# Hedgehog attention and a ReGLU FFN on one Trainium2 core: gates between load bursts and crossbar turns, w_phi loaded by SyncE, and matmuls on zeros early on

## The chip, the cores and the metric

One NeuronCore of a Trainium2 chip runs the whole kernel. The metric is device time in microseconds (us) of one execution. The engines are TensorE (PE; PEld are its weight loads), VectorE (DVE), ScalarE (ACT), GpSimd (POOL) and SyncE (SP, which here only issues DMAs). Each engine works through its own list of instructions in order.

## What is computed

Attention with a learned feature map, over 8 batches of 8 heads, 576 positions and head dimension 64, and then a gated feed-forward net over all 4608 tokens:

```python
def phi(x):                                   # w_phi: 64 x 128
    proj = einsum('bhsd,df->bhsf', x, w_phi)
    proj = proj - max(abs(proj), axis=-1, keepdims=True)
    return concatenate([exp(proj), exp(-proj)], axis=-1)
q_p, k_p = phi(q), phi(k)
kv  = einsum('bhsf,bhsd->bhfd', k_p, v);  z = sum(k_p, axis=2)
num = einsum('bhsf,bhfd->bhsd', q_p, kv)
den = einsum('bhsf,bhf->bhs', q_p, z)[..., None] + 1e-06
x = (num / den)                               # to 4608 x 512
out = (maximum(x @ w_gate, 0) * (x @ w_val)) @ w_out     # 512 -> 1536 -> 512
```

Inputs and output are fp32; the kernel multiplies in bf16.

## The kernel before

**Stages.** For each batch the kernel loads k, q and v. The first 512 positions of a head are the "main" part (tiles kn, qn, vn), the last 64 are the "rest" (km, qm, vm). k and q must be turned (transposed) so that the head dimension lies on partitions. Batches 0 and 1 are turned on TensorE (`turn_pe`, L439, copied out of PSUM at L446), the others by DMA transposes through the crossbar, issued by SyncE (`turn_dma`, L454). TensorE projects the turned k with w_phi (L493 for pairs of heads, L539 for the rest). VectorE takes the largest magnitude of each row (L503), ScalarE the two exponentials (`exps`, L467). Since exp(proj - m) is exp(proj) times exp(-m), the k maxima are put on v instead: GpSimd scales v by them (`vs`, L518; rest `vsm`, L559, which for batch 0 can also go to VectorE). TensorE forms kv (`k_kv`, L586), with a column of scales beside v so that z comes with it. q is projected (L610), its maxima are found (L619; for batch 0 by a second projection with positions on partitions, L679, and a reduction L686), and q times kv is formed in `q_num` (L717). VectorE adds the two halves (L725, L732), takes the reciprocal (L742), GpSimd or VectorE divides (`xu`, L745), and xu is turned to xT (batch 0 on TensorE, L758 and L765, the others by SyncE).

**FFN.** There are nine groups: one for the main part of each batch, and a last one for all rests (`xT_mix`). Each group has 12 slices of the hidden dimension. For each, TensorE makes val (L787 with wv_sb) and gate (L787 with wg_sb), ScalarE copies val out of PSUM (L793), VectorE makes relu(gate) * val (L796). Then 4 x 12 products with wo_sb (L818) make four output tiles, copied at L828 and stored by SyncE at L833 (L837 for the rests). PSUM has 8 banks, handed out in a ring named `ps`.

**Order of the work.** Nothing runs in the order of the code. Every step is an `Op` with an engine or a choice of engines, an assumed duration, dependencies, buffers, and a key by which it ranks. `Plan.run` (L91) is a list scheduler that runs on the host when the program is built: it steps through assumed time, gives each free engine the ready step with the smallest key, and the order that comes out is the order in which each engine's instructions are written. Its assumptions decide only this order; on the chip semaphores decide when an instruction starts. Assumed durations, the added delays `LAT` and the factor of 1.8 on TensorE before `COLD` (L61, L173) are such assumptions.

**Loads and gates.** Loads of batch 0's k and v are issued by SyncE (L372, L386), the other loads mostly by GpSimd, which can convert fp32 to bf16 on the way. Batch 0's k arrives as fp32 in the space of wo_sb and is cast at L871: heads 0-1, 2-3, 4-7 and then the rest. w_phi is loaded twice by GpSimd (L335) into the two diagonal blocks of `w2`, whose other blocks VectorE clears (L341). Loads of batches 2 to 7 and all crossbar turns are marked `alone`: the planner starts a load only when it believes that SyncE's transfers have ended, and a turn only when it believes that GpSimd's have. A turn has besides a real wait (`gate`, set at L180, written at L1102) on the last GpSimd load planned before it. GpSimd's loads have no such wait on the turns. Loads of batch 0's q and of the first third of the FFN weights wait for k heads 4-7 (L895 to L902).

Of the kernel before, what the change touches and what calls it, by code (L numbers as in the profile page):

```python
# [18 lines left out]
class Buf:  # L19


    __slots__ = ("ring", "slot", "users", "free_at", "lock", "place")

    def __init__(self, ring):
        self.ring, self.slot, self.users, self.free_at, self.lock = ring, None, 0, 0.0, 0.0
        self.place = ring.made
        ring.made += 1
# [13 lines left out]
class Op:  # L41
    __slots__ = ("eng", "dur", "fn", "deps", "bufs", "banks", "key", "kind", "start", "end",
                 "land", "succ", "left", "ready", "bytes", "pad", "n", "inst", "alone", "gate", "tail", "bias")

    def __init__(self, eng, dur, fn, deps, bufs, banks, key, kind, nbytes, pad):
# [6 lines left out]
        self.succ, self.left, self.ready = [], 0, 0.0  # L52


class Plan:
# [3 lines left out]
    LAT = {PE: 0.26, ACT: 0.16, DVE: 0.2, POOL: 0.15, SP: 0.1}  # L59
    MARGIN = 0.2  # L60
    COLD = 14.0  # L61
# [29 lines left out]
    def run(self, quota):  # L91
        wait = {e: [] for e in (PE, ACT, DVE, SP, POOL)}
# [4 lines left out]
        last_load = None  # L97
# [9 lines left out]
        events = [0.0, 0.25, 0.75]  # L107
        order = []
        while left:
# [7 lines left out]
            while progress:  # L117
                progress = False
                for e in wait:
# [3 lines left out]
                    for o in wait[e]:  # L123
                        if o.start is not None or (best and o.key >= best.key):
                            continue
                        r = o.ready
# [5 lines left out]
                        if any(b.lock > now + 1e-9 for b in o.banks):  # L132
                            continue
# [20 lines left out]
                        if ok:  # L154
                            best = o
                    if best is None:
                        continue
# [15 lines left out]
                    if e == PE and now < self.COLD:  # L173
                        d *= 1.8
# [4 lines left out]
                    if o.alone and e == SP:  # L179
                        o.gate = last_load  # L180
# [11 lines left out]
                    for b in o.banks:  # L192
                        b.lock = o.land
# [10 lines left out]
                    for s in o.succ:  # L204
                        s.ready = max(s.ready, o.land)
                        s.left -= 1
                        if not s.left:
                            release(s)
                            heapq.heappush(events, max(s.ready, now))
# [12 lines left out]
def kernel(  # L222
# [16 lines left out]
    P = 128  # L239
# [68 lines left out]
    w2 = single("w2", [P, 2, F])  # L308

# [8 lines left out]
    op = plan.op  # L318

# [13 lines left out]
    def load_w():  # L333
        for hh in range(2):
            nc.gpsimd.dma_start(out=w2[D * hh : D * (hh + 1), hh, :], in_=w_phi)  # L335

    o_w = op(POOL, 1.3, load_w, key=(0, 0), pad=2.2)

    def clear_w():
        for hh in range(2):  # L340
# [40 lines left out]
    def load_rest_by_head(b, src, engname, key, tile_buf, deps=(), pad=0.0, dst=None):  # L381
        def go():
            v_ = src[b, :, SF:S, :].rearrange("(j x) p d -> x p j d", x=2)
            t = tile_buf.t if dst is None else dst
            for x in range(2):
                i = engines[engname].dma_start(out=t[SM * x : SM * (x + 1)], in_=v_[x])  # L386
            return i
# [5 lines left out]
    def load_rest_q(i, key, tile_buf, deps=(), pad=2.0):  # L393
        def go():
            for x in range(2):
                ins_ = nc.gpsimd.dma_start(
# [3 lines left out]
            return ins_  # L400
# [8 lines left out]
    SWITCH = 0.12  # L409
# [74 lines left out]
    def k_item(b, u, kT, turned, vn, o_v, key, dve_scale=False):  # L484
# [4 lines left out]
        def rows():  # L489
            for i in range(4):  # L490
# [7 lines left out]
        a = op(PE, 0.224 + SWITCH, rows, [*turned(2 * u), *turned(2 * u + 1), o_w],  # L498
               [kT, kp, m, e, vs], pair,
               key, "a")  # L500
        for x, ps in enumerate(pair):
# [31 lines left out]
    def k_rest(b, kmT, turned, vm, o_v, key, dve_scale=False):  # L533
# [22 lines left out]
        for x in range(2):  # L556
# [11 lines left out]
            sc.append(op(engs, {POOL: 1.12, DVE: 0.8}, scale, [o_e, o_v, o_clear], [vm, e, vs],  # L568
# [31 lines left out]
    def q_cols(hq, qT, turned, cols, dsts, mx, mdst, key):  # L600
# [6 lines left out]
        def go_cols():  # L607
            for x in range(2):
# [3 lines left out]
        a = op(PE, 0.222 + SWITCH, go_cols, [*turned, o_w],  # L612
               [qT, *{id(d[0]): d[0] for d in dsts}.values(), *([mx] if mx else [])], pair, key, "a")
        reds, exd = [], []
# [14 lines left out]
    def q_scale(mq, xq, zq, cq, n, deps, key):  # L629
# [34 lines left out]
        a = op(PE, 0.25, away, [*deps, o_consts], [mq, xq, zq, cq], [ps], key, "a")  # L664
        r = op(DVE, 0.2, amax, [a], [mq, xq], [ps], key, "a")
        z = op(DVE, 0.2, spread, [r, o_consts], [xq, zq], key=key, kind="a")
        b_ = op(PE, 0.2, back, [z], [zq], [ps], key, "a")
# [192 lines left out]
    W = C * D  # L860

# [16 lines left out]
    k_heads = ((0, 2), (2, 4), (4, 8))  # L878
    for i, (lo, hi) in enumerate(k_heads):
        o = load_main(0, "kn", k, SP, slice(lo, hi), (0, i), None, (), 0.0, kn32)  # L880
        last_k = o
        for u in range(lo // 2, hi // 2):
            c_ = cast(
                kn32[:, 2 * u : 2 * u + 2], lambda u=u: ins[0]["kn"].t[:, 2 * u : 2 * u + 2], 2 * W,
                [o], (2, 0, 0, u), ins[0]["kn"], (DVE, ACT),
            )
            got["kn", 0, 2 * u] = got["kn", 0, 2 * u + 1] = c_
    o = load_rest_by_head(0, k, SP, (0, 3), None, (), 0.0, km32)
    got["km", 0] = cast(km32, lambda: ins[0]["km"].t, NU * D, [o], (2, 0, 0, 5), ins[0]["km"],
# [247 lines left out]
```

## Time and profile before

| | |
|---|---|
| median of 4 runs | 405.69 us (405.07, 415.23, 404.29, 406.31) |
| the profiled execution | 405.07 us, of which its span is 403.3 us |
| TensorE clock granted over the span | 0.995 |
| busy: PE, DVE, ACT, POOL | 372.7, 262.0, 241.9, 165.3 us |
| FFN products L787 (wv, wg) and L818 | 95.6, 96.7 and 100.5 us |
| HBM read, written | 37.81 MB, 9.44 MB |

Times in the profile are counted from the span's start. "Busy" counts time in which at least one instruction of that engine was under way; matmuls overlap, so a group's busy time is less than its count times its mean. "Chain" is the chain of work that ended last, followed back from the end. A wait names the instruction that waited, what released it, and the total, the number of times and the longest, in us. In the timeline a row is a start, a length, an engine, a line and an operation with its count. A DMA's time to landing runs from its issue to its completion.

### The profile page before, as it was taken

How to read it: one execution, taken by the hardware profiler on the slowest of the kernel's cores; microseconds unless marked ns; L12 is line 12 of the kernel's file. 1: busy time of each engine (PE TensorE's matmuls, PEld its weight loads, DVE VectorE, ACT ScalarE, POOL GpSimd, SP SyncE). 2: the span in 40 equal slices, each digit the busy share in tenths (PEclk: the TensorE clock that was granted, in tenths of full speed). 3: DMA queues.
4: the chain of work that ended last, by engine and by line, in shares of the span. 5: the costliest groups of instructions: out<-in, count | busy, mean ns of one | idle time of the engine just before them, and what ended most of it. 6: DMA issues, size and time to landing. Idle time of an engine off the chain costs nothing.

```text
span 403.3 us, 8431 instructions
## 1 busy us (share of the span) xinstructions
PE 372.7 (92%) x3149; PEld 199.8 (50%) x3149; DVE 262.0 (65%) x648; ACT 241.9 (60%) x522; POOL 165.3 (41%) x196
## 2 busy tenths in 40 slices
PE   3687899989999999999899899989999999999995
PEld 2365588543643545364365436533654444444442
DVE  5879888298677789978975997378775311321420
ACT  5969985179639849878662795279713323323321
POOL 4864953149539625954963197345031000000000
PEclk9999899999999999999999999999999999999999
DMA  8999199490959964798696809581042001002004
GB/s 229 164 226 209 34 161 225 103 181 2 222 112 165 154 166 88 131 125 190 106 161 179 159 15 156 152 174 43 2 105 66 2 37 69 0 13 93 1 1 104
DMA packets 86217, 45.60 MB, mean 113 GB/s; under 512 B 57824, under 2 KB 78816, under 8 KB 86176
## 3 DMA queue, kind: packets, MB, share of 16 engines
q0 software_dynamic: 29472, 20.68, 31.6%
q1 hardware_dynamic: 56704, 24.39, 27.8%
q8 instruction: 24, 0.39, 0.4%
q14 instruction: 17, 0.14, 0.1%
HBM read 37.81 MB, written 9.44 MB: 117 GB/s over the span
## 4 chain that ended last, share of the span: by engine, by line
PE 76%; DMA 11%; DVE 4%; ACT 3%; issue 2%; SPq 1%; POOL 1%; DVEq 0%; ACTq 0%
PE ps L787 42%; PE ps L818 20%; DMA kT<-kn 5%; PE ps L586 5%; PE ps L717 4%; PE ps L610 3%; DMA vm<-in_v_dram 2%; ACT kp L467 2%; DMA qn<-in_q_dram 2%; DMA wo_sb<-in_k_dram 1%; PE ps L493 1%; SPq L454 1%; DMA qT<-qn 1%; DVE mk L503 1%; PE ps L656 1%
## 5 line engine op out<-in xcount | busy, mean ns | idle before, releaser
L796 DVE SCALAR_TENSOR_TENSOR h<-ps,val 128x512 bf16<-128x512 f32 (+1 forms) x120 | 75.3, 631 | 76.4 <-PE ps L787 74.0
L793 ACT CAST val<-ps 128x512 bf16<-128x512 f32 (+1 forms) x120 | 69.3, 579 | 59.5 <-PE ps L787 54.5
L787 PE MATMUL ps<-xT,wv_sb 128*128 128x512 bf16 (+1 forms) x432 | 95.6, 357 | 5.5 <-ACT xT L765 1.9
L818 PE MATMUL ps<-wo_sb,h 128*128 128x512 bf16 x432 | 100.5, 379 | 0.0
L787 PE MATMUL ps<-xT,wg_sb 128*128 128x512 bf16 (+1 forms) x432 | 96.7, 358 | 0.3 <-ACT kp L467 0.2
L745 POOL TENSOR_TENSOR xu<-u,r 128x512 bf16<-128x512 f32 x35 | 36.4, 1042 | 111.1 <-DVE r L742 57.2
L467 ACT ACTIVATE qp<-ps 128x512 bf16<-128x512 f32 x144 | 78.8, 692 | 5.1 <-PE ps L610 2.6
L467 ACT ACTIVATE kp<-ps 128x512 bf16<-128x512 f32 x128 | 71.6, 632 | 12.8 <-PE ps L493 11.0
L518 POOL TENSOR_TENSOR vs<-vn,ek 128x1024 bf16<-128x1024 f32 x32 | 61.5, 1921 | 23.1 <-PE ps L493 6.3
L787 PEld LDWEIGHTS <-wv_sb 128*128 128x128 bf16 x480 | 45.4, 98 | 48.9 <-issue 7.7
L787 PEld LDWEIGHTS <-wg_sb 128*128 128x128 bf16 x480 | 44.4, 99 | 41.7 <-issue 3.5
L818 PEld LDWEIGHTS <-h 128*128 128x128 bf16 x432 | 39.9, 98 | 44.9 <-issue 1.9
L828 ACT COPY ob<-ps 128x512 f32<-128x512 f32 x30 | 17.6, 587 | 66.0 <-PE ps L818 61.7
L503 DVE TENSOR_REDUCE mk<-ps 128x4 f32<-128x512 f32 x64 | 40.5, 668 | 2.8 <-PE ps L493 2.7
L725 DVE TENSOR_TENSOR t<-ps,cq 128x195 f32<-128x195 f32 (+1 forms) x84 | 24.2, 327 | 22.8 <-PE ps L717 22.3
L619 DVE TRANSPOSE_TENSOR_REDUCE mq<-ps 128x16 f32<-128x512 f32 x56 | 36.1, 688 | 2.5 <-PE ps L610 2.5
L732 DVE TENSOR_TENSOR u<-ps,t 128x195 f32<-128x195 f32 (+3 forms) x120 | 35.3, 329 | 1.0
L717 PEld LDWEIGHTS <-qp 128*128 128x128 bf16 x640 | 27.1, 98 | 11.5 <-issue 1.7
L717 PE MATMUL ps<-kv,qp 128*128 128x65 bf16 x640 | 29.9, 193 | 0.6 <-DVE u L732 0.3
L586 PEld LDWEIGHTS <-kp 128*128 128x128 bf16 x512 | 23.1, 102 | 5.3 <-DVE mr L686 2.5
L586 PE MATMUL ps<-vs,kp 128*128 128x65 bf16 x512 | 23.8, 200 | 2.0 <-DVE mr L686 2.0
L586 PE MATMUL ps<-vsm,kpm 128*128 128x65 bf16 x128 | 21.6, 199 | 0.0
(89 smaller groups left out, 298.5 us busy)
## 6 DMA issues: line engine op xcount, KB each, us to landing
out_dram<-ob SPq DMA_DIRECT2D x32, 256.0 KB, 2.5
vn<-in_v_dram POOLq DMA_DIRECT2D x6, 1024.0 KB, 10.5
qn<-in_q_dram POOLq DMA_DIRECT2D x8, 512.0 KB, 8.2
kn<-in_k_dram POOLq DMA_DIRECT2D x7, 512.0 KB, 6.2
wo_sb<-in_moe_w_out_dram POOLq DMA_DIRECT2D x1, 1536.0 KB, 13.9
vn<-in_v_dram SPq DMA_DIRECT2D x2, 512.0 KB, 6.4
vn<-in_v_dram SPq DMA_DIRECT2D x1, 1024.0 KB, 5.6
wv_sb<-in_moe_w_val_dram POOLq DMA_DIRECT2D x1, 1024.0 KB, 12.9
```

What stands on the lines that cost most here:

```text
L467: nc.scalar.activation(dst(s), ps.t.rearrange("p (c f) -> p c f", f=f), AF.Exp, scale=sign)
L503: nc.vector.tensor_reduce(m.t.rearrange("p (i x) -> p x i", x=2)[:, x], ps.t.rearrange("p (c f) -> p c f", f=F), axis=AX.X, op=ALU.max, ap ...
L518: eng.tensor_tensor(vs.t[:, :, :, 0:D], vn.t[:, 2 * u : 2 * u + 2].rearrange("p h c d -> p (h c) d")[:, :, None, :] .to_broadcast([P, 2 * ...
L586: nc.tensor.matmul(acc[:, hh, s, :], lhsT=lhsT, rhs=rhs, start=(n == 0), stop=(n == 19))
L619: nc.vector.tensor_reduce(mdst(x), ps.t.rearrange("p (h j t) -> p h j t", j=NQ, t=32), axis=AX.X, op=ALU.max, apply_absolute_value=True, a ...
L717: nc.tensor.matmul(ps.t[:, E * (2 * i + s) : E * (2 * i + s + 1)], lhsT=qp.t[:, s, h, :], rhs=kv_of[b][h // 2][0].t[:, h % 2, s, :],)
L732: nc.vector.tensor_tensor(u.t[rows, lo : lo + n], ab[:, :, 0], t.t[rows, 0:n], op=ALU.add)
L745: eng.tensor_tensor(xu.t, u.t[:, :, 0:D], r.t.to_broadcast([P, H, D]), op=ALU.mult)
L787: nc.tensor.matmul(ps.t[:, 0:n], lhsT=w[:, dc, P * fi : P * fi + P], rhs=xt()[:, dc, lo:hi], start=(dc == 0), stop=(dc == NDC - 1),)
L793: nc.scalar.copy(val.t[:, 0:n], pv.t[:, 0:n])
L796: nc.vector.scalar_tensor_tensor(h.t[:, fi, lo:hi], pg.t[:, 0:n], 0.0, val.t[:, 0:n], op0=ALU.max, op1=ALU.mult,)
L818: nc.tensor.matmul(ps.t, lhsT=h.t[:, fi, P * t : P * t + P], rhs=wo_sb[:, fi, :], start=(fi == 0), stop=(fi == NFC - 1),)
```

## The change

Five things change together. w_phi is loaded once, as fp32, by SyncE, right behind k heads 0-1, by one DMA that reads it twice (an outermost step of 0) into both halves of a new tile `w32`; VectorE casts it into `w2`. The rest of batch 0's k is loaded ahead of heads 4-7, and its casts may also go to GpSimd. A GpSimd load that is marked `alone` gets a real wait on the last SyncE turn planned since the last such wait, as turns had on loads; where a load or turn consists of several DMAs, the first of them now waits, on the last of the other. Where the planner finds TensorE idle between 1.3 and 24 us of its assumed time it writes a 128x128 matmul of a tile of zeros into the last PSUM bank, which nothing else may use until then. And the planner's assumptions change: the cold time is 5.5 instead of 14, projections of 64 rows count as another mode of TensorE (0.06 for a switch, and a preference for the same mode, instead of 0.12 on each), results for the same engine count as ready earlier, a PSUM bank no longer waits out the added delay for the same engine, VectorE's vsm price is 1.9 instead of 0.8.

In the built program TensorE's list has 119 matmuls on zeros: 32 ahead of the first turn, 88 ahead of the turns of q, the last ones among batch 0's q products. Nine GpSimd loads have the new wait: k of batch 2, k and km of batch 3, k of batch 4, k and v of batch 5, vm of batch 6, k and v of batch 7.

```diff
     RATE = {POOL: 320.0, SP: 290.0}
     LAT = {PE: 0.26, ACT: 0.16, DVE: 0.2, POOL: 0.15, SP: 0.1}
+    SAME = {PE: 0.0, ACT: 0.1, DVE: 0.1, POOL: 0.15, SP: 0.1}
     MARGIN = 0.2
-    COLD = 14.0
+    COLD = 5.5
+    SWITCH = 0.06
+    WARM = (1.3, 24.0)
+    STICK = 1.0
...
                     for o in wait[e]:
-                        if o.start is not None or (best and o.key >= best.key):
+                        key = o.key
+                        if e == PE and o.mode and o.mode == mode:
+                            key = (*key[:2], key[2] - self.STICK)
+                        if o.start is not None or (best and key >= best_key):
                             continue
-                        r = o.ready
+                        r = o.ready.get(e, 0.0)
...
-                        if any(b.lock > now + 1e-9 for b in o.banks):
+                        if any(b.lock > now + 1e-9 and b.by != e for b in o.banks):
                             continue
...
                     if best is None:
+                        if e == PE and self.WARM[0] <= now < self.WARM[1]:
+                            free[e] = now + 0.11
+                            heapq.heappush(events, free[e])
+                            w = Op(PE, 0.11, self.warm, [], [], [], (99,), "w", 0, 0.0)
+                            w.start, w.end, w.land = now, free[e], free[e]
+                            order.append((now, len(order), w, e))
                         continue
...
                     if o.alone and e == SP:
-                        o.gate = last_load
+                        o.gate, last_turn = last_load, o
+                    if o.alone and e == POOL:
+                        o.gate, last_turn = last_turn, None
                     if o.bytes and e == POOL:
                         last_load = o
...
                     for s in o.succ:
-                        s.ready = max(s.ready, o.land)
+                        for en in s.eng:
+                            at = o.land
+                            if en == e and not o.bytes and not o.pad:
+                                at = o.end + self.SAME[e]
+                                heapq.heappush(events, at)
+                            s.ready[en] = max(s.ready.get(en, 0.0), at)
...
+    warm_bank = R["ps"].tiles[-1]
+    R["ps"].free[len(R["ps"].tiles) - 1] = Plan.WARM[1] + 0.2
+
+    def warm():
+        nc.tensor.matmul(warm_bank[:, 0:P], lhsT=zero, rhs=zero)
...
     def load_w():
+        two = bass.AP(tensor=w_phi.tensor, offset=w_phi.offset, ap=[[0, 2], [F, D], [1, F]])
+        return nc.sync.dma_start(out=w32, in_=two)
+
+    def cast_w():
         for hh in range(2):
-            nc.gpsimd.dma_start(out=w2[D * hh : D * (hh + 1), hh, :], in_=w_phi)
-
-    o_w = op(POOL, 1.3, load_w, key=(0, 0), pad=2.2)
+            rows_ = slice(D * hh, D * (hh + 1))
+            nc.vector.tensor_copy(w2[rows_, hh, :], w32[rows_])
+
+    o_w32 = op(SP, 0.53, load_w, key=(0, 0.5), kind="l", nbytes=2 * D * F * 4)
+    o_w = op(DVE, 0.3, cast_w, [o_w32], key=(2, 0, -30.0))
 
     def clear_w():
+        nc.vector.memset(zero, 0.0)
...
-        a = op(PE, 0.224 + SWITCH, rows, [*turned(2 * u), *turned(2 * u + 1), o_w],
+        a = op(PE, 0.224, rows, [*turned(2 * u), *turned(2 * u + 1), o_w],
                [kT, kp, m, e, vs], pair,
                key, "a")
+        a.mode = 1
...
-            sc.append(op(engs, {POOL: 1.12, DVE: 0.8}, scale, [o_e, o_v, o_clear], [vm, e, vs],
+            sc.append(op(engs, {POOL: 1.12, DVE: 1.9}, scale, [o_e, o_v, o_clear], [vm, e, vs],
                          key=key, kind="a"))
...
+    CAST = (POOL, ACT, DVE)
...
     k_heads = ((0, 2), (2, 4), (4, 8))
+    o_km = load_rest_by_head(0, k, SP, (0, 1.5), None, (), 0.0, km32)
+    got["km", 0] = cast(km32, lambda: ins[0]["km"].t, NU * D, [o_km], (2, 0, 0, 5), ins[0]["km"],
+                        CAST)
     for i, (lo, hi) in enumerate(k_heads):
         o = load_main(0, "kn", k, SP, slice(lo, hi), (0, i), None, (), 0.0, kn32)
...
-    o = load_rest_by_head(0, k, SP, (0, 3), None, (), 0.0, km32)
-    got["km", 0] = cast(km32, lambda: ins[0]["km"].t, NU * D, [o], (2, 0, 0, 5), ins[0]["km"],
-                        (DVE, ACT))
...
+        if o.bytes or o.gate is not None:
+            o.inst = o.inst if isinstance(o.inst, list) else [o.inst]
         if o.gate is not None:
-            tc.add_manual_dep(o.inst.ins, o.gate.inst.ins.name, sync, reason="turns behind loads")
+            tc.add_manual_dep(o.inst[0].ins, o.gate.inst[-1].ins.name, sync,
+                              reason="turns and loads apart")
```

## The prediction

> **What bounds the kernel now.** I read the page first, then stage windows, then TensorE's waits, then the timeline of the first 30 us, then the queues' own instructions.
>
> ```profile
> span 403.3 us, 8431 instructions
> PE 372.7 (92%) x3149; PEld 199.8 (50%) x3149; DVE 262.0 (65%) x648; ACT 241.9 (60%) x522; POOL 165.3 (41%) x196
> ...
> PE   3687899989999999999899899989999999999995
> ...
> PEclk9999899999999999999999999999999999999999
> ...
> PE 76%; DMA 11%; DVE 4%; ACT 3%; issue 2%; SPq 1%; POOL 1%; DVEq 0%; ACTq 0%
> ```
>
> TensorE is the bound: 372.7 of 403.3 us busy, so at most 30.6 us are to be had. The slices show that much of this lies at the start. Stage windows (columns: stretch, length, busy PE, PEld, DVE, ACT, POOL with counts, clock, DMA, GB/s) place it:
>
> ```profile
> 0.00:5.00 5.00, 0.62 (x5) 0.36 (x6) 2.86 (x10) 2.59 (x4) 2.24 (x9) 1.00 0.53 156
> 5.00:10.00 5.00, 3.09 (x30) 2.08 (x30) 2.17 (x5) 3.19 (x7) 2.15 (x3) 1.00 1.08 303
> 10.00:15.00 5.00, 2.44 (x26) 1.68 (x27) 4.75 (x13) 4.85 (x14) 3.65 (x4) 1.00 1.33 191
> 15.00:20.00 5.00, 3.79 (x21) 1.75 (x18) 3.92 (x6) 4.73 (x10) 5.00 (x6) 1.00 0.86 143
> 20.00:25.00 5.00, 3.53 (x62) 3.43 (x62) 3.94 (x8) 1.78 (x5) 5.00 (x8) 1.00 0.96 262
> 25.00:30.00 5.00, 4.44 (x53) 2.71 (x52) 3.13 (x6) 5.00 (x12) 1.50 (x2) 1.00 1.50 184
> ```
>
> With the rows up to 50 us (3.87, 3.30, 8.01) PE is busy 33.1 of the first 50: 16.9 idle. From 390 to the end 5.05 are idle (last copies and stores, untouched). The other 8.65 lie between. In the start ScalarE, not PE, is full (4.85, 4.73, 5.00), except for 3.22 us in 20:25. Who PE waits for (total, times, longest):
>
> ```profile
> PE ps L493 <- DMA kT<-kn: 4.1, 4, 1.5
> PE ps L586 <- DVE mr L686: 2.0, 1, 2.0
> ...
> PE ps L610 <- DMA qT<-qn: 1.4, 2, 0.7
> ...
> PE ps L493 <- DMA w<-in_w_phi_dram: 1.1, 1, 1.1
> ```
>
> So w_phi costs a wait at 5.8 us, the turns of k and q cost 5.5 us later, and at 19.5 to 21.5 PE's kv products (L586) stand behind a PSUM bank that VectorE's q maxima still hold. Two rows of the chain in order of time show an early and a late kv run:
>
> ```profile
> 21.47 3.48 PE ps L586 x60
> ...
> 102.81 1.22 PE ps L586 x40
> ```
>
> 58 ns a product early, 30 ns later.
>
> **What the Trainium skill says.** "TensorE: Matmul & The Clock Gate", part 1 (the HAM clock gate): the array runs at half clock until a window of about 3.4 us has been busy. The trace agrees on the half (58 against 30 ns), though the clock row says 9 there. "DMA: Bandwidth & Descriptors", why a DMA increments its semaphore by 16: the number of engines used is the largest up to 16 that divides the outermost dimension of both sides. The new w_phi read has an outermost repeat of 2, so two engines would carry all 128 rows; the trace of before has no such load. The same page, queues and rings: one queue's rows run in ring order on each engine, so what SyncE issues next stands behind them. "SBUF — State Buffer", terms: VectorE and GpSimd share a port pair that one holds for a whole instruction; the trace agrees with the direction, L559's two halves taking 1.14 and 2.30 us, the second beside GpSimd's L518.
>
> **The change part by part.** The profiled execution took 405.07 us for a span of 403.3; the sum is made against 405.07. The median of the four runs, 405.69, is 0.6 above because of one run of 415.23; I add nothing for that.
>
> *w_phi and km.* Two GpSimd loads go (1.24 us of POOL before the identity; nobody waited for POOL there). SyncE issues the new load second: later SyncE loads move by about 0.5 us of issue. k heads 2-3 and, now that km's two issues (1.43) precede them, k heads 4-7 come after it: the latter's issue moves from 1.75 to about 3.7. w_phi is 64 rows of 512 B on each of two engines. k moved at about 296 GB/s at 2 to 4 us, 55 ns per 1 KB row and engine; by bytes 64 rows cost 28 ns each, 1.8 us. Upper bound: k heads 4-7 took 3.4 us after heads 2-3 for 32 rows an engine, 106 ns a row, 6.8 us. Lower bound: 1.1 us, if two engines alone run faster. I take 1.8. Then heads 0-1 end on those engines near 3.1, w_phi lands near 5.3, heads 2-3 near 6.2 (before about 4.2), k heads 4-7 near 9 to 9.8 (before 7.6). VectorE's order is w cast, cast of heads 2-3, both kT copies: it waits in order, so the first k rows run at about 7.2 and the first exponential at 7.5 instead of 8.11: 0.6 earlier. The q load is gated on heads 4-7, goes at 9.5 instead of 7.85 and lands near 15.8 instead of 14.2.
>
> *The new order of the first batch.* Up to the first product of q and kv (L717, at 28.67) ScalarE needs from its first exponential at 8.11 to 28.2, less idle 0.15, 0.27 and 3.22: about 16.4 us of work. In the new order PE has two kv products ahead of the q rows, so the 2.0 us wait behind L686 and ScalarE's 3.2 idle go; VectorE takes the k casts and kT copies, ScalarE the second q copy, about equal. 7.5 + 16.4 + 0.7 waiting for q = 24.6. The other leg is GpSimd: vs at 12 to 16.2, one vsm half 1.8 (VectorE's 2.30 gone), then k loads of batch 1 (2.2, formerly behind all vs), then two more vs at 2.15 each and a copy of 0.7: 25.3, kv product and copy to 26.3. That leg is last. 28.67 - 26.3 = 2.4 us earlier. Bounds: 4 earlier if w_phi hides in other engines' lag, 0.3 later at 106 ns a row.
>
> *Matmuls on zeros.* 119 pairs, 88 of them ahead of the q turns, placed where PE would be idle. At half clock a pair costs about 113 ns (16 turns in 1.89 us at 14.20), so the first 32 take 3.6 us from about 1.1: to 4.7, where the first k cast ends at 4.2: 0.5 late at most, and hidden, since kT's copy now waits for 6.2. Their own cost is nothing while PE idles; without that cover 119 x 0.06 = 7 us. Their gain: 80 kv products save 28 ns each, 2.2 us, of which most is already in the two kv legs above (ScalarE's wait ended by them); I count nothing more.
>
> *Batch 1 and FFN begin.* k of batch 1 is issued some 1 to 4 us earlier, q of batch 1 at about 25.4 instead of 22.71, behind the vs. It landed 9.2 later; with k already out of the way I take 7 to 8, so 32.4 to 33.4, and PE's in-order turn of it stands before the second half of batch 0's q products. Needed near 33.92 - 2.4 = 31.5: 0.6 given back of a possible 0 to 2.
>
> *Load gates.* Nine GpSimd loads now wait for a SyncE turn. Queued behind them on POOL are vs (L518), xu (L745) and the other loads; behind those kv products and xT turns. In before one burst ran into turns: k turns issued at 171.13 while q, qm and v loads were issued from 172.00; the chain holds that turn for 9.89 us from 172.47 (median 3.3) and PE lost 1.1. That goes: -1.1. Most other turns already waited for whole bursts, so they gain nothing. New cost: a gated load holds POOL for what is left of a turn, 0 to 3.3 us; POOL is 59% idle. I take +0.1, net -1.0, bounds -3 (half of the 5.5) to +3 outside the rival below.
>
> *Prices and tie rules of the planner* (cold time, mode switch, same-engine latency) only reorder: PE's list has the last q product after 840 of 1296 FFN products of full width instead of 856, so the FFN tail still ends the kernel and a shift at the start reaches the end in full. 0, bounds 1 each way.
>
> Sum: -2.4 + 0.6 - 1.0 = -2.8, **402.3 us**.
>
> **The rivals.** *The gain is used up at the start (0.25).* At 106 ns a row, less some 1.3 us by which two engines may run ahead, heads 4-7 land at 13.1, q at 19.1, q copies end at 21.7, then kp 2.2, and q exponentials 5: 28.9, as before. Or the zeros do not raise the clock. Left: +0.2 + 0.6 - 1.0: 404.9. For: ring order. Against: 296 GB/s with 1 KB rows. *Slower: turns and loads take turns in a ring (0.21).* Turns already wait for the last load (SyncE stood 99.4 us for vm); now loads wait for the last turn, with vs and xu locked behind. PE already waits for k and q turns six times, so it has no slack there: every microsecond that a burst is held reaches PE. If half of the six bursts are held by a full turn (3.3), less the 1 us that POOL can spare, and the next turns follow: 3 x 2.3 = 6.9, 405.07 - 1.8 + 6.9 = 410. It decides from about 0.7 us a burst on. Against: POOL's idle 59%, and the planner orders with the same gates.
>
> **How the numbers follow.** Forecast 0.54, its own range 398.5 to 404. Under 398 0.05, over 408 about 0.13: range 398 to 408. 0.5% is about what a measurement of this kernel tells from no change: 403.7 and 407.7. Forecast below 403.7 plus under 398: faster 0.55; the used-up case and the forecast's edge: same 0.23; slower 0.22.
>
> **What would show it.** First L763 (old L717) near 26.3; first exponential near 7.5, not 6 or 9; kv at 30 ns a product from its first run; ScalarE's hole in 20:25 gone; idle PE from 50 to 390 near 7.6. Wrong, if the first q products start after 28.7 (w_phi's two engines), or if idle from 50 to 390 grows beyond 11 with POOL waiting on DMA ahead of vs and xu.

## The result and the profile after

The changed kernel took 410.15 us (median of 34 runs, 405.98 to 413.99). The kernel before, run in turns with it on the same chips, took 407.79 us (55 runs). The ratio is 1.0103, with a 95% interval of 1.0082 to 1.0124: slower by about 1%, where 402.3 us was forecast, and above the top of the range (408). Ratios here and below leave out slow executions, those over 1.5% above the fastest of the same kernel (here 27 of the 55 and 4 of the 34); the two medians, over all runs, are 0.6% apart. The profiled execution took 409.03 us for a span of 407.3. Beside the kernels of the experiments the median of the kernel before lay between 407.2 and 410.0 us, so below only ratios to it on the same chip are given, with their intervals.

The page of the changed kernel, four of its lines. Lines of code have moved: L439 is now L483, L493 is L537, L586 is L631, L518 is L563, L648 is L694, L656 is L702, L871 is L918, L787 is L833, L717 is L763.

```profile
span 407.3 us, 8667 instructions
...
PE 381.0 (94%) x3268; PEld 208.8 (51%) x3268; DVE 291.4 (72%) x685; ACT 224.5 (55%) x486; POOL 166.0 (41%) x196
...
PEclk9789899989999999999969999999999999999998
...
PE 77%; DVE 13%; ACT 4%; DMA 2%; issue 1%; SPq 0%; POOL 0%; DVEq 0%; POOLq 0%
```

DMA has gone from 11% of the chain to 2%: of TensorE's waits for turns of k and q (4.1 and 1.4 us before) 1.3 us is left. VectorE stands there instead, with 13% for 4%. Its busy time has grown by 29 us. Some 17 of these may be work that ScalarE no longer does (224.5 for 241.9); the rest calls for a cause. The clock row has a 6 in the slice from 204 us. TensorE's waits say which two VectorE instructions it is (total, times, longest):

```profile
PE ps L483 <- DVE kn L918: 7.1, 2, 5.6
PE ps L702 <- DVE zq L694: 6.2, 2, 5.6
...
PE ps L537 <- DMA kT<-kn: 1.3, 1, 1.3
```

First the cast of k heads 4-7 (`kn`), in the timeline of 5 to 20 us:

```profile
11.06 5.43 DVE L918 CAST kn<-wo_sb 128x512 bf16<-128x512 f32 x2
11.13 0.77 POOL L461 DMA_DIRECT2D wg_sb<-in_moe_w_gate_dram  x1
...
11.89 1.94 POOL L563 TENSOR_TENSOR vs<-vn,ek 128x1024 bf16<-128x1024 f32 x1
...
13.89 1.93 POOL L563 TENSOR_TENSOR vs<-vn,ek 128x1024 bf16<-128x1024 f32 x1
...
16.17 0.61 PE L483 MATMUL ps<-ident,kn 128*128 128x128 bf16 x4 [5.64 <-DVE kn L918]
```

Two casts, priced at 0.43 each, take 5.43 us. The first of them alone takes 5.04: it begins while GpSimd still issues a load and ends 0.3 us after GpSimd's second v scaling. TensorE stands 5.64 us. Then, in the timeline of 180 to 212 us, the spread of the q maxima (`zq`, 0.29 us in the kernel before):

```profile
181.45 1.04 POOL L791 TENSOR_TENSOR xu<-u,r 128x512 bf16<-128x512 f32 x1 [2.26 <-DVE r L788]
...
189.46 0.95 POOL L416 DMA_DIRECT2D vn<-in_v_dram  x1 [6.97 <-DMA xT<-xu]
...
196.62 1.94 POOL L563 TENSOR_TENSOR vs<-vn,ek 128x1024 bf16<-128x1024 f32 x1
...
198.88 6.91 DVE L694 TENSOR_TENSOR zq<-xq,one_a 128x128 f32<-128x128 f32 x1
...
204.61 1.03 POOL L604 TENSOR_TENSOR vsm<-vm,ekm 64x512 bf16<-64x512 f32 x1
```

Read it from the second line. The load of batch 5's v has one of the nine new waits and holds GpSimd for 6.97 us. What SyncE still had to issue when that wait began, at 182.49, is in its own list:

```profile
182.81 2.53 SPq L498 DMA_TRANSPOSE xT<-xu  x2
185.44 1.21 SPq L498 DMA_TRANSPOSE qmT<-qm  x1
186.74 1.22 SPq L498 DMA_TRANSPOSE xT<-xu  x1
```

The other loads that stand behind the held one, and a division, go out until 196.6, and only then come the v scalings of batch 5, four in a row (196.62, 198.62, 200.62, 202.61). In the kernel before the first of them began at 189.34, with divisions between some of them. The spread starts inside the second and ends 6.91 us later, after the fourth and after the first scaling of the rest (`vsm`); TensorE stands 5.61 us. The stage windows show the price of that stretch (TensorE's busy time, and after the other engines its clock):

```profile
200.00:210.00 10.00, 4.39 (x13) 1.79 (x12) 7.09 (x3) 1.80 (x6) 7.07 (x10) 0.67 0.65 167
```

After the stall the products of 512 columns follow each other at 427 ns instead of 216 until about 210. "TensorE: Matmul & The Clock Gate", section on HAM oscillation, gives a gap of about 3.4 us as the length from which the array goes back to half clock. The runs of this study agree for longer gaps: half rate follows each of the gaps of 3.5, 3.9, 4.9, 5.2 and 5.6 us in their traces. Shorter ones are below.

To see what the rest of the change did, I priced every matmul in the trace, zeros apart, at 0.421 ns per column (216 ns for 512) and took the time that had passed less the work done. This lag, in us:

| at | 30 | 50 | 200 | 210 | end |
|---|---|---|---|---|---|
| before | 20.0 | 28.2 | 38.6 | 39.5 | 50.8 |
| after | 20.3 | 28.2 | 37.7 | 45.8 | 54.8 |

The whole loss lies between 200 and 210: 8.1 us there (5.6 idle, the rest half clock) where the kernel before loses 0.9. Outside that stretch the changed kernel is 3.2 us better. But the start, from which I took most of my gain, gave none: at 50 us both have 28.2.

### The profile page after: what moved, and what is told of

Same layout as the page of the kernel before. It is cut to its first block, busy times and chain, and to the rows that moved or that the text cites. A ratio compares the mean times of both kernels' runs of the same rounds, so it can differ in the third digit from the quotient of the medians.

```text
span 407.3 us, 8667 instructions
## 1 busy us (share of the span) xinstructions
PE 381.0 (94%) x3268; PEld 208.8 (51%) x3268; DVE 291.4 (72%) x685; ACT 224.5 (55%) x486; POOL 166.0 (41%) x196
## 4 chain that ended last, share of the span: by engine, by line
PE 77%; DVE 13%; ACT 4%; DMA 2%; issue 1%; SPq 0%; POOL 0%; DVEq 0%; POOLq 0%
PE ps L833 39%; PE ps L864 23%; PE ps L631 4%; PE ps L763 4%; DVE mk L548 3%; DVE zq L694 2%; DVE u L778 2%; DVE t L771 2%; PE ps L655 2%; ACT kp L511 1%; DVE h L842 1%; ACT qp L511 1%; DVE kn L918 1%; PE ps L537 1%; ACT val L839 1%
## 5 line engine op out<-in xcount | busy, mean ns | idle before, releaser
L842 DVE SCALAR_TENSOR_TENSOR h<-ps,val 128x512 bf16<-128x512 f32 (+1 forms) x120 | 75.2, 630 | 53.8 <-PE ps L833 50.8
L833 PE MATMUL ps<-xT,wv_sb 128*128 128x512 bf16 (+1 forms) x432 | 102.4, 363 | 1.1 <-DVE xT L811 0.4
L833 PE MATMUL ps<-xT,wg_sb 128*128 128x512 bf16 (+1 forms) x432 | 102.1, 361 | 0.1
L563 POOL TENSOR_TENSOR vs<-vn,ek 128x1024 bf16<-128x1024 f32 x32 | 61.1, 1910 | 21.4 <-PE ps L833 15.3
L833 PEld LDWEIGHTS <-wg_sb 128*128 128x128 bf16 x480 | 45.4, 100 | 43.5 <-issue 4.6
L833 PEld LDWEIGHTS <-wv_sb 128*128 128x128 bf16 x480 | 44.9, 99 | 43.3 <-issue 4.7
L874 DVE COPY ob<-ps 128x512 f32<-128x512 f32 x29 | 19.9, 686 | 34.4 <-PE ps L864 34.4
L778 DVE TENSOR_TENSOR u<-ps,t 128x195 f32<-128x195 f32 (+3 forms) x120 | 36.4, 329 | 2.2 <-POOL xu L791 0.9
L763 PEld LDWEIGHTS <-qp 128*128 128x128 bf16 x640 | 28.3, 98 | 12.1 <-issue 1.5
L763 PE MATMUL ps<-kv,qp 128*128 128x65 bf16 x640 | 31.6, 193 | 0.3 <-DVE u L778 0.2
L631 PEld LDWEIGHTS <-kp 128*128 128x128 bf16 x512 | 21.3, 98 | 2.9
L631 PE MATMUL ps<-vs,kp 128*128 128x65 bf16 x512 | 22.0, 193 | 0.0
L631 PE MATMUL ps<-vsm,kpm 128*128 128x65 bf16 x128 | 20.3, 193 | 0.0
```

The lines of the kernel that those rows point to most:

```text
L563: eng.tensor_tensor(vs.t[:, :, :, 0:D], vn.t[:, 2 * u : 2 * u + 2].rearrange("p h c d -> p (h c) d")[:, :, None, :] .to_broadcast([P, 2 * ...
L631: nc.tensor.matmul(acc[:, hh, s, :], lhsT=lhsT, rhs=rhs, start=(n == 0), stop=(n == 19))
L763: nc.tensor.matmul(ps.t[:, E * (2 * i + s) : E * (2 * i + s + 1)], lhsT=qp.t[:, s, h, :], rhs=kv_of[b][h // 2][0].t[:, h % 2, s, :],)
L778: nc.vector.tensor_tensor(u.t[rows, lo : lo + n], ab[:, :, 0], t.t[rows, 0:n], op=ALU.add)
L833: nc.tensor.matmul(ps.t[:, 0:n], lhsT=w[:, dc, P * fi : P * fi + P], rhs=xt()[:, dc, lo:hi], start=(dc == 0), stop=(dc == NDC - 1),)
L842: nc.vector.scalar_tensor_tensor(h.t[:, fi, lo:hi], pg.t[:, 0:n], 0.0, val.t[:, 0:n], op0=ALU.max, op1=ALU.mult,)
```

## The experiments

Two explanations stood against each other. *Ports:* VectorE's casts and its spread are held off by GpSimd's scalings, wherever these fall. *Gate:* the new waits hold GpSimd, and what is queued behind it comes late; the slow spread is only how that shows.

**VectorE's two operations rewritten.** The cast as a reduction over an axis of length one, the spread with its operand left in PSUM, two forms that, if *Ports* holds, do not wait for GpSimd.

```diff
+            if eng is nc.vector:
...
+                eng.tensor_reduce(d_, s_[:, :, None], axis=AX.X, op=ALU.add)
+                return
...
-                xq.t[0:cols], ps.t[0:cols, 0:P].rearrange("p (g t) -> p t g", g=NQ),
+                ps.t[0:cols, 2 * P : 2 * P + 32],
+                ps.t[0:cols, 0:P].rearrange("p (g t) -> p t g", g=NQ),
...
-                xq.t[0:cols][:, None, :].to_broadcast([cols, NQ, 32]),
+                ps.t[0:cols, 2 * P : 2 * P + 32][:, None, :].to_broadcast([cols, NQ, 32]),
```

*The cast alone.* 

> The changed kernel with one edit: VectorE's casts of the first k from fp32 to bf16 are written as a reduction over an axis of length 1, on the same engine, at the same places. Theory (port): the cast of 5.04 us at 11.06 was kept from SBUF by GpSimd's loads and vs products, through the port pair the two engines share[...]; a reduction does not. Then it takes about 0.65 us, PE's wait of 5.6 us behind it falls to 1 us or less, and the time falls by some 4 us from the changed kernel, to about 0.0% against the kernel before. Rival (late data): the cast was waiting for k heads 4-7, late behind w_phi on two DMA engines; then it stays near 5 us and the time stays 1% over before.

*The spread alone.* 

> The changed kernel with one edit: the q scales' maxima (xq) are kept in PSUM, in unused columns of the bank that they were read from, so that VectorE's spread into zq reads one operand from SBUF instead of two. Theory (port): the spread of 6.91 us at 198.88 was held off while GpSimd ran four vs products in a row; with one SBUF operand it takes 0.3 us each of the seven times, PE's wait of 5.6 us near 200 us goes, and the time falls by 4 to 6 us from the changed kernel. Rival (load gates): PE's hole near 200 us comes from turns and loads that wait for each other, so it stays at 4 to 6 us, only put down to another cause, and the time stays 1% over before.

*Both.* 

> Both edits in the changed kernel. Theory (port): the two stalls are independent, both go, about 10 us of PE idle are won back with a little more for a clock that does not fall: near 400 us, 1.3% to 2% faster than the kernel before. If the mechanism that I forecast (start 2 us earlier, fewer waits for turns) is real, this is where it shows: first q products near 26 us, idle from 50 to 390 us near 4. Rival: what one stall gave up, the next wait takes; then the time lies within 0.5% of before.

*Both, and w_phi by two loads of 64 rows, spread over 16 engines.* 

> Both edits, and w_phi loaded by two DMAs of 64 rows each instead of one DMA with an outermost repeat of 2. Theory: the one DMA runs on two of sixteen DMA engines, lands 4.6 us after its issue and holds up the k rows queued behind it on these two. With two DMAs on all engines it lands near 4.2 us instead of 5.8, k heads 2-3 near 5 instead of 6.5, the first exponential starts near 6.6 instead of 7.9, in spite of 0.5 us more of issue on SyncE; the time is 0.5 to 1.2 us less than with both edits alone. Rival: the landing is late for the HBM traffic around it; then nothing moves by more than 0.3 us, or it gets later by the extra issue.

Measured: 1.0031 (1.0007 to 1.0055), 1.0032 (0.9994 to 1.0069), 0.9987 (0.9949 to 1.0026) and 1.0014 (0.9985 to 1.0043). So the forms matter, but both together only bring the kernel back to where it was (the rival of that expectation, not the 1.3% to 2% of the port theory), and w_phi on 16 engines adds nothing at the end. The kernel with both shows why, in TensorE's waits:

```profile
PE ps L631 <- POOL vsm L610: 3.4, 2, 2.6
```

The spread is quick again (0.29 us), and TensorE now waits near 205 us for the scalings of the rest, the last that GpSimd makes there. The idle time of 200 to 230 fell from 5.6 only to 3.6, half rate follows for 3 us, and the lag over 200 to 210 still grows by 5.5 us. That is the gate's account: GpSimd itself is late.

The kernel with the spread alone rewritten shows something else, at the start. Its cast of k heads 4-7 has the form of the changed kernel and began at the same time (11.07), and yet took 0.38 us, and the first q products came at 25.4. GpSimd was 0.7 us later there, with its first scaling at 12.60 instead of 11.89. So whether that cast is held seems to turn on tenths of a microsecond; that rests on one trace.

**All nine waits taken away**, in the order as written:

```diff
-        if o.gate is not None:
+        if o.gate is not None and not (o.alone and e == POOL):
```

*From the changed kernel.* 

> The changed kernel with the same written order, without the waits of GpSimd loads on crossbar turns; both slow VectorE operations stay as they are. If the load of batch 5's v that held GpSimd for 6.97 us is what bunches the four v scalings near 197 us, and these starve the spread: the spread's longest run falls below 1.5 us, TensorE's idle in 200 to 230 falls from 5.6 to about 1 to 2 us, and the ratio to the kernel before falls from 1.010 to about 1.000 (the slow cast at 11 us stays, 5 us). If the bunching comes from the planner's order alone: the spread still takes 5 to 7 us and the ratio stays at 1.010. If the waits were worth something by keeping loads and turns apart: a turn of over 5 us appears and the ratio is 1.012 or more.

*From the kernel with both operations rewritten.* 

> Both VectorE operations rewritten as before (ratio 0.999 with the waits in place), and now without the waits of GpSimd loads on turns. If the held GpSimd is what is left near 205 us (TensorE waited 2.6 us for vsm there): that wait goes, TensorE's idle in 200 to 230 falls from 3.6 to about 1, and the ratio is 0.990 to 0.994. If loads among turns cost as much as the waits do: idle moves to another stretch, ratio 0.997 to 1.001.

*The same with w_phi on 16 engines.* 

> The candidate for the best version: both VectorE operations rewritten, w_phi in two loads of 64 rows each on all 16 engines, no waits of GpSimd loads on turns. If the parts add: 0.990 to 0.994 from the missing waits and another 0.5 to 1 us from the earlier first exponential (7.2 instead of 7.9), ratio 0.988 to 0.992. If the late q loads, 2.5 us each in batches 0 and 1, take up what w_phi gives: same ratio as the kernel with two engines for w_phi, within 0.002.

Measured: 1.0055 (0.9996 to 1.0114), 0.9981 (0.9927 to 1.0035), 1.0027 (0.9964 to 1.0091). The first lies between what I had named for the gate (1.000) and for the other cases (1.010 and more), and its trace shows what took the wait's place, in the division that stands between batch 5's v load and the scalings:

```profile
193.08 1.04 POOL L791 TENSOR_TENSOR xu<-u,r 128x512 bf16<-128x512 f32 x1 [4.61 <-DMA xT<-xu]
```

The v load went out at 184.10, a turn of xT at 184.37, among the loads; that turn landed 8.5 us later, where such a turn took 2.4 to 2.5 in the changed kernel. The division waits for it, and the scalings begin at 195.93, still late. The spread takes 3.4 us, and the lag over 200 to 210 grows by 3.1 us.

The second kernel met the rival I had written down for it: idle time moves. In 200 to 230 it fell to 0.2 us, and in 230 to 260 it rose to 5.7. The timeline of 230 to 252 us of this second kernel:

```profile
234.38 3.41 SPq L498 DMA_TRANSPOSE kT<-kn  x2
...
236.47 0.95 POOL L416 DMA_DIRECT2D vn<-in_v_dram  x1
237.96 2.35 SPq L498 DMA_TRANSPOSE kmT<-km  x1
...
245.57 0.61 PE L584 MATMUL ps<-w,kmT 128*128 128x256 bf16 x2 [5.21 <-DMA kmT<-km]
```

The load of batch 7's v, 1 MB, begins between two turns, and TensorE stands 5.2 us for the second. With its wait in place (both operations rewritten, all waits) that load stood 9.0 us in GpSimd's queue, until the turns of k and q and a turn of qmT behind them had landed, and the turn of kmT cost TensorE at most 0.9. In the changed kernel this load is held the longest of all, 7.8 us, and TensorE is idle for 0.9 us in 230 to 260. So the nine waits are not alike, and the length of a hold is not its price.

**The waits alone, in the kernel before.**

```diff
...
-                        o.gate = last_load
+                        o.gate, last_turn = last_load, o
+                    if o.alone and e == POOL:
+                        o.gate, last_turn = last_turn, None
...
```

As in the change, where a load or turn consists of several DMAs the first waits on the last of the other.

> The kernel before with one part of the change alone: GpSimd loads marked alone wait for the last turn planned ahead of them, in the order of the kernel before. If the waits cost by themselves: GpSimd shows waits on DMA of 3 us or more ahead of a v scaling or a division, ratio 1.005 to 1.010. If my forecast of this part was right in itself (a gain of 1.0 us from the burst at 172 us, no loss): ratio 0.996 to 0.999 and the longest turn falls from 9.9 to some 3 us. If the waits do harm only in the changed kernel's order: 1.000.

Measured: 0.9979 (0.9939 to 1.0020). No GpSimd wait on a turn shows ahead of a scaling or a division, and the turn that took 9.9 us from issue to landing takes 3.9. But the q load of that burst now goes out at 180.37 instead of 172.00, and TensorE stands 3.5 us for a turn of q at 197 us. In that order of work the waits do neither harm nor good that can be measured.

**One wait of the nine taken away:** that of batch 5's v.

```diff
-        if o.gate is not None:
+        if o.gate is not None and not (o.alone and e == POOL and o.key[1] == 5 and o.key[2] == 3):
```

*From the kernel with both operations rewritten, and again on another chip.* 

> Both VectorE operations rewritten; of the nine waits of GpSimd loads on turns only one goes, that of batch 5's v, which held GpSimd for 6.8 us before it came to the v scalings. Without all nine, TensorE's idle in 200 to 230 fell to 0.2 us but a turn of kmT that met batch 7's v load took 5.2 us from TensorE near 245. If that is the whole account: idle in 200 to 230 stays near 0.3 and in 230 to 260 it is 1 to 2, idle from 50 to 380 is 7.5 to 9.5, the span is 399 to 402 us, ratio 0.988 to 0.994. If other collisions take their place: idle from 50 to 380 stays at 11 to 13 and the ratio at 0.998.

> The fastest so far once more, beside the other two on one chip: 0.987 to 0.995.

*The same with w_phi on 16 engines.* 

> As the kernel without batch 5's wait, and w_phi loaded in two parts of 64 rows on 16 engines: the candidate for the best. If the start reaches the end: 0.5 to 1.5 us less than the kernel with two engines for w_phi. If the late q loads take it up: the same within 0.002.

*From the changed kernel, with nothing else touched.* 

> The changed kernel as it is, both slow VectorE operations included, without the one wait of batch 5's v load. If that wait made the bunch of four scalings that the spread ran into: the spread's longest falls from 6.9 to some 2 us, TensorE's wait for it from 5.6 to about 2, the ratio from 1.010 to 1.001 to 1.004; the cast of 5 us at 11 us stays. If the two VectorE operations are the whole account and the wait only matters with them gone: ratio 1.008 or more.

Measured: 0.9909 (0.9865 to 0.9953) and again 0.9869 (0.9807 to 0.9931); with w_phi on 16 engines 0.9938 (0.9906 to 0.9970); from the changed kernel **0.9885** (0.9833 to 0.9938). The last is the decisive run, and it beat what I expected of it (1.001 to 1.004). One wait less turns 1.0103 into 0.9885, its span is 400.2 us instead of 407.3, and the VectorE operations have the form that the change gave them. The two ratios differ by 2.2%, some 8.9 us, and the spans by 7.1; the ratios come from different chips, and each span is one execution. The kernel without that wait, its stretch and its spreads (shortest, median and longest, in ns):

```profile
200.00:210.00 10.00, 9.95 (x145) 6.42 (x144) 6.83 (x17) 4.58 (x11) 3.01 (x5) 1.00 0.69 112
```

```profile
L694 DVE TENSOR_TENSOR zq<-xq,one_a x7: 291/293/2225, 53.6 to 260.2; 128x128 f32<-128x128 f32 x7
```

The scalings start at 191.51 instead of 196.62, still four in a row: that they bunch comes from the new order, that they come late from the wait. The last of them is 0.3 us from its end when the spread begins, at 199.08; the spread takes 0.47 us instead of 6.91 (the longest of the line, 2.2 us, is another spread, which takes as long in the changed kernel). The lag over 200 to 210 grows by some 0.7 us instead of 8.1. The turns now meet the loads here too and land up to 8.8 us after their issue, but the one that the division waits for was issued 0.3 us ahead of the v load and landed in time. The cast at 11 us is as slow as before (5.1 us for the two), and yet the ratio is what it is. Rewriting the two operations on top of this (0.9909 and 0.9869) adds nothing that can be measured. The four kernels without this wait (one of them measured twice, one in the next experiment) lie at 0.986 to 0.994, and each is faster than its like with all nine.

**Without the matmuls on zeros**, in the order as written:

```diff
-    plan.warm = warm
+    plan.warm = lambda: None
```

> Both VectorE operations rewritten, the order as written, and the 119 matmuls on zeros left out. My forecast gave them no cost and most of a 2.2 us gain at the first kv products: then the kv products of batch 0 start at 58 ns each instead of 30 and the first q product moves later by 0.5 to 2 us, ratio 1.000 to 1.004. If the zeros delay real work instead (the first 32 pairs end at 4.6 us, before any k is there, the others stand before q turns): the first q product moves earlier, ratio 0.995 to 0.998. If they are hidden and useless: ratio 0.999, as with them.

> The fastest so far (both VectorE operations rewritten, one wait less, 0.991) without the matmuls on zeros. If they are hidden and useless: the same ratio within 0.003 of the one with them in this call. If they raise the clock for the first kv products: 0.5 to 2 us slower. If they stand before real work: 0.5 to 1 us faster.

Measured: 1.0004 (0.9970 to 1.0038) with all waits, against 0.9987 with the zeros; without batch 5's wait 0.9861 (0.9811 to 0.9910), against 0.9869 with them on the same chip. Without the zeros the first half of batch 0's kv products stand 55 ns apart, with them 30 (35 in the kernel with all waits). That is 40 products by 25 ns, 1.0 us, and it doesn't reach the end. The second half stands 30 to 33 ns apart without zeros too, against 54 in the kernel before: that part came from the new order. Nor do the zeros always do what they are for. With w_phi on 16 engines and the zeros in place, the first half stood 54 and 55 ns apart in two traces, in which TensorE had just waited 2.5 and 3.9 us for q.

**VectorE's operations measured by themselves.** None of the reference is computed; four of each form in a row, alone and beside GpSimd's work.

```diff
+            nc.gpsimd.tensor_tensor(
+                vs[i][:, :, :, 0:64],
+                vn[:, :, None, :].to_broadcast([P, 8, 2, 64]),
+                e[:, :, :, None].to_broadcast([P, 8, 2, 64]),
+                op=ALU.mult,
+            )
...
+            nc.vector.tensor_copy(cd[i], src)
...
+            nc.vector.tensor_reduce(rd[i], src[:, :, None], axis=AX.X, op=ALU.add)
...
+            nc.vector.tensor_tensor(
+                zd[i], xq[:, None, :].to_broadcast([P, 4, 32]),
+                one[:, :, None].to_broadcast([P, 4, 32]), op=ALU.mult,
+            )
```

The fourth form is the last one with its operand in PSUM. The second measurement puts `nc.gpsimd.tensor_copy(vs[i][:, :, :, 64], e)` behind each scaling.

> None of the reference is computed: four forms of VectorE operation, four of each in a row, alone, then beside four v scalings of 128x8x2x64 on GpSimd, then beside four GpSimd load issues. If GpSimd's two-operand operation holds what VectorE needs for a whole instruction: alone the cast takes 0.4 us and the spread 0.3; beside the scalings the first cast and the first spread take 2 us or more, the one with most bad luck the length of all four scalings (7 to 8 us), while the reduction of one operand (0.67) and the spread from PSUM (0.3) stay as they are. If the slow ones came from DMA traffic or issues: nothing changes beside the scalings, and beside the issues the cast takes 1 us or more.

> None of the reference is computed: the four forms of VectorE operation again, now beside four v scalings on GpSimd each followed by the copy of the 128x16 column of scales, as in the kernel. Measured without that copy, a cast and a spread waited for one scaling each (1.9 to 2.1 us), no more; in the changed kernel the cast took 5.0 and the spread 6.9, which is two and four scalings. If the short copy between the scalings is what keeps VectorE out: the first cast and the first spread take 7 us or more. If not: 2 us each, as without it, and the length in the kernel has another cause.

The first one's timeline (start, length of the four together):

```profile
2.50 1.42 DVE L76 CAST cd<-src 128x512 bf16<-128x512 f32 x4
...
9.54 8.23 DVE L76 CAST cd<-src 128x512 bf16<-128x512 f32 x4
...
18.13 2.45 DVE L81 TENSOR_REDUCE rd<-src 128x512 bf16<-128x512 f32 x4
...
25.69 7.61 DVE L86 TENSOR_TENSOR zd<-xq,one 128x128 f32<-128x128 f32 x4
...
33.66 0.87 DVE L94 TENSOR_TENSOR pd<-xp,one 128x128 f32<-128x128 f32 x4
...
41.21 2.16 DVE L76 CAST cd<-src 128x512 bf16<-128x512 f32 x4
```

Alone, four casts take 1.42 us and four spreads 0.89. Beside four scalings of 1.9 us each they take 8.23 and 7.61: each waits for one scaling. The reduction (2.45) and the spread from PSUM (0.87) take what they take alone. Beside GpSimd's load issues (the last line) four casts take 2.16, a bounded cost. This is what "SBUF — State Buffer", section on who interferes with whom, states form by form. It says that the loser blocks for the other's whole instruction; here that was one instruction at a time, 2.1 us at most, and not the length of all four that I had allowed for. The second measurement, with the short copy between the scalings as in the kernel, gave the same 2.1 us:

```profile
L87 DVE TENSOR_TENSOR zd<-xq,one x8: 282/1105/2134, 7.1 to 32.7; 128x128 f32<-128x128 f32 x8
```

So why in the kernel the cast, which began 0.8 us ahead of the first scaling, waited until two were over, and the spread for four instructions, stays open. The short copy isn't the reason.

## Why the prediction was wrong, step by step

**w_phi and km: right within some 0.5 us.** The cast of w_phi began at 5.85 us, as it landed (forecast 5.3), the cast of heads 2-3 at 6.5 (6.2), the first exponential came at 7.86 (7.5, so 0.25 us were won instead of 0.6), the q load went at 9.32 (9.5). The two engines do cost: on 16 the cast of w_phi began at 4.2 to 4.4 and the first exponential came at 7.2 and 7.4 in the two of these kernels that keep waits. But this brought nothing measurable at the end.

**The new order of the first batch: wrong, and without weight.** "VectorE takes the k casts and kT copies, ScalarE the second q copy, about equal" priced the casts at 0.43. Beside the scalings they took 5.43 us, and the first q products came at 29.04 instead of 26.3. I had named the shared port pair and pointed at a scaling on VectorE slowed by it, and yet priced these casts as if they ran alone. With the reduction in their place the first q products came at 24.0 to 27.8, and at 25.4 in the trace in which the cast itself was not held. But that gain did not arrive either: the kernels with one wait less end the same with the slow casts as with the quick ones. TensorE's largest wait in the second run with the rewritten operations, and a window of its clock:

```profile
PE ps L483 <- DMA qn<-in_q_dram: 4.5, 2, 3.9
```

```profile
36.00:38.00 2.00, 2.00 (x21) 1.39 (x19) 1.55 (x5) 1.45 (x5) 1.36 (x2) 0.50 1.13 213
```

It waits 3.9 us for q of batch 1, which lands at 32.3 us, by luck as forecast (32.4 to 33.4): it was issued at 23.4 instead of 25.4 and took 9.0 us instead of 7 to 8. But TensorE needs it at 28.5, not at 31.5, and then runs at half rate until 38. I gave back 0.6 of 2.4 for this; in that execution nearly all goes. With 2.4 us of that wait, in the first run of the same kernel, the lag at 50 us was 25.5 instead of 27.7. What the start is worth thus hangs on when one load lands.

**Matmuls on zeros: right in the sum, half right in the cause.** They count for nothing at the end, as the sum said. All 80 kv products did run at 30 ns, but of the 2.2 us that I gave to the zeros the runs without them show 1.0.

**Load gates: the step that failed.** "A gated load holds POOL for what is left of a turn, 0 to 3.3 us; POOL is 59% idle. I take +0.1." Three things were wrong in it. The wait isn't for what is left of a turn under way. It is for a turn that SyncE may not yet have issued. When the v load came to wait, at 182.5 us, two xT turns, one of qmT and a third xT turn were still to be issued. The third went at 186.74, xT turns landed 2.4 us after their issue there, and GpSimd went on at 189.46: by these times the third is the one that the load waits for. In the trace six of the nine loads are held, for 1.1 to 7.8 us, three of them for longer than the 3.3 us that I had as the most. Second, an engine that is idle 59% of the time isn't idle where the wait falls: the scalings of batch 5 came 7 us later than in the kernel before, and TensorE, which works in order too, stood at the product that needs the spread. Third, a stall of this length is paid twice, first idle, then at half clock. With this one wait the kernel takes 1.0103, without it 0.9885; I had put the whole cost of the waits at 0.1 us. The step's other half, a gain of 1.1 us, can't be read by itself. Outside 200 to 210 us the change is worth 3.2 us, none of it from the start, and the kernel without any of these waits is slower (1.0055) than the one with eight (0.9885). But in the order of the kernel before the waits alone gave no gain that can be measured (0.9979, 0.9939 to 1.0020).

**The rival** "turns and loads take turns in a ring" said 410 us, by POOL held and vs and xu locked behind. That is the mechanism, and the time within 1 us. Its sum was another one, though: three bursts by 2.3 us, where it was one wait, by its two consequences, for 7.1 us of span. Its sign, POOL waiting on DMA ahead of vs, was there; its mark of 11 us idle in 50 to 390 wasn't reached (9.7): time at half clock doesn't count as idle. So the right total is in part luck.

**The planner's prices** were taken at nothing. No run tells them apart from the rest of the new order: what they did is in the 3.2 us, and in the bunch of four scalings.

## What to carry to other kernels

Before a wait is put on an in-order engine, price it by the issue list of the queue that it waits for, up to the named transfer, and ask what stands behind the waiting instruction just there: in this order of work eight such waits together were worth having, and the ninth cost more than all the rest gained. A stall is dear from the length at which TensorE loses its clock, so that one long stall costs more than its idle time. And where loads and turns meet, tenths of a microsecond can decide who waits, so one trace of a kernel doesn't show what its next execution does. Where VectorE works beside GpSimd, look at the form: a cast in SBUF or two operands from SBUF waited for GpSimd here, a reduction or an operand in PSUM didn't.

## What the runs showed that I had not expected

The cast waited 5.0 us and the spread 6.9 in the kernel for instructions of 1.9 us each, while measured alone no such wait was over 2.1. Half rate followed some shorter gaps as well: one of 2.3 us at 148 us in one run and none of 2.2 at 124 in another, and after 1.4 us near 40 us in some executions and not in others. The length of one gap alone doesn't decide it below 3.5 us. A reduction over an axis of length one casts 128x512 fp32 to bf16 in 0.67 us whatever GpSimd does, against 0.42 for a cast alone and 2.1 beside a scaling. And the fastest kernels of the study, at 0.986 to 0.991 of the kernel before, differ from one another in casts, spread and zeros by nothing that could be measured; what they all lack is the one wait.
